# A retention and mixer kernel: batch 0 in the layout of the other batches, k turned back on TensorE, w2 cast by its DMA

## The chip, the core and the metric

The kernel runs on one core of a Trainium2 chip. A core has five engines with queues of their own: TensorE (PE; its weight loads are shown as PEld), VectorE (DVE), ScalarE (ACT), GpSimd (POOL) and SyncE (SP, which here only starts loads). Data lie in SBUF; matmuls write to PSUM, which has eight banks of 2 KB for each of 128 partitions. The metric is the device time of one execution in microseconds (us), as the median of several runs. The profile shows one execution of its own; times inside it count from the start of its span.

## What is computed

Four batches of 768 tokens with eight heads of width 64. A retention layer, written as a recurrence over the tokens, gives y; it is laid out as x with 512 columns. Then a low-rank mixing over the tokens is added, and a two-layer MLP with 2048 hidden columns:

```python
for t in range(S):
    state = gamma * state + k[:, :, t] (outer) v[:, :, t]
    y[:, :, t] = scale * q[:, :, t] @ state          # scale = 1/sqrt(64)
x = y.transpose(0, 2, 1, 3).reshape(B, S, H * D)
h = x.transpose(0, 2, 1) @ U @ V                     # rank 32
u = x + h.transpose(0, 2, 1)
out = u + relu(u @ w_ch1) @ w_ch2
```

Inputs and output are float32; the kernel multiplies in bf16 and accumulates in float32.

## The kernel before

**Retention by chunks.** A batch is cut into six chunks of 128 tokens. The decay is folded into q and into k or v as powers of gamma, so a chunk needs three products: scores of k against q within the chunk (masked to the causal part by DVE), the running state of k against v (kept in a PSUM bank "st" and copied to bf16 for the next chunk), and mix, which adds q times the state to the masked scores times v. Its result, x, is evacuated by ACT.

**Two layouts.** Batch 0 takes the first one: `prep_chunk` (L231) casts a chunk of q, k and v on POOL, `turn` (L266) transposes q and k on TensorE into a bank of PSUM, ACT copies them out as qkT, `score` (L293) and `mix` (L306) follow. Batches 1 to 3 take the head-pair layout: q and k are loaded with 32 partitions for each pair of heads and eight adjacent tokens in a partition (`feed_one`, L121, four DMAs of 128 KB for a tile of 256 tokens), cast by POOL (L211 and L215), and transposed in blocks of 32 by DVE (`turn_block`, L327). `score4` (L337) and `mix4` (L372) then work with a contraction over 32 partitions, four of them side by side. These batches also load k in its natural layout (L103), because the state needs tokens on the partitions.

**PSUM.** R (L63) is one tile of four banks, used by the retention and by the low-rank step; three banks "mlp" take turns in the MLP; one bank holds the state.

**Order.** The order of all instructions is written out by hand. SP starts the loads in the order of the list `feed` (L137 to L151); `take` and `feed_one` start the next load as one is used, with 19 tiles in flight at first. For batch 0 the loop at L519 runs turn of chunk ci, the casts of the next chunk, mix of chunk ci - 1 and score of chunk ci. Next come the casts of w1, the transposes of x for the first 512 tokens, the low-rank step (`lr_proj`, its copy pc on DVE, a product with V at L540, four evacuations to uT), and then the MLP of batch 0, whose first instruction is a matmul of L451. POOL meanwhile casts the first block of batch 1 and all of w2.

The MLP of a batch is a list of pieces: 16 up pieces of 512 tokens, 16 of 256 tokens (L451, with relu on ACT or DVE), and 24 down pieces of four matmuls each (L474). Every fourth down piece ends with an addition on DVE (L479) and a store, which POOL issues (L440). `weave` (L488) strews the next batch's retention and low-rank step between these pieces, at the shares of the total that stand in `AT` and `LR` (L551 to L557): for each block of 256 tokens the transposes, scores, mix, scores, mix; then projection (L403), sum (`lr_expand`, L412 and L419), and two turns of u into uT (`lr_turn`, L428, evacuated by ACT). All four read and write R.

Of the kernel before, what the change touches and what calls it, by code (L numbers as in the profile page):

```python
# [9 lines left out]
fp32 = mybir.dt.float32  # L10
# [3 lines left out]
ENG = mybir.EngineType  # L14
# [3 lines left out]
def kernel(  # L18
# [11 lines left out]
    nc = tc.nc  # L30
# [9 lines left out]
    RING = 19  # L40
    NBK = S // 256
    NST = 4
# [21 lines left out]
    Rb = R.bitcast(bf16)  # L64
# [28 lines left out]
    def feed_chunk(b, ci):  # L93
        for nm, src in (("q", q), ("k", k), ("v", v)):
            feed.append(((nm, b, ci),
                         src[b, :, ts(ci, P), :].rearrange("h p d -> p h d")))

    def feed_block(b, bk):
        for nm, src in (("qT", q), ("kT", k)):
            feed.append(((nm, b, bk), src[b, :, ts(bk, 256), :]))  # L100
        for ci in (2 * bk, 2 * bk + 1):
            for nm, src in (("k", k), ("v", v)):
                feed.append(((nm, b, ci),  # L103
                             src[b, :, ts(ci, P), :].rearrange("h p d -> p h d")))
# [32 lines left out]
    for ci in range(NCK):  # L137
        feed_chunk(0, ci)
# [4 lines left out]
    feed_block(1, 0)  # L143
    for m in range(NM):
        feed.append((("w2", m), moe_w_ch2[ts(m, P)]))
    for b in range(1, B):
        for bk in range(NBK):
            if (b, bk) != (1, 0):
                feed_block(b, bk)
    for _ in range(RING):  # L150
        feed_one()  # L151


    lg = consts.tile([P, NCK, H], fp32)
# [9 lines left out]
    for h in range(H):  # L164
        nc.vector.memset(lg[:, :, h], math.log(gammas[h]))
    nc.vector.tensor_tensor(pos, pos, lg, op=ALU.mult)
    gq = consts.tile([P, NCK, H], fp32)
    gk = consts.tile([P, NCK, H], fp32)
    nc.scalar.activation(gq, pos, AF.Exp)
    nc.scalar.activation(gk, pos, AF.Exp, scale=-1.0)  # L170
    nc.vector.tensor_scalar(gq, gq, 1.0 / math.sqrt(D), None, op0=ALU.mult)
# [4 lines left out]
    states = []  # L176
    for i in range(NST):
        t = consts.tile([P, 4, P], bf16, name=f"state{i}")
        nc.vector.memset(t, 0.0)
        states.append(t)  # L180

    def causal(t):
        return t[:, None, :].to_broadcast([P, 4, P])


    gqT = consts.tile([P, NBK, 8, 2], fp32)

    def make_gqT():
        lgT = consts.tile([P, NBK, 2, 8], fp32)
        posT = consts.tile([P, NBK, 2, 8], fp32)  # L190
        for hp in range(4):
            r = ds(32 * hp, 32)
            nc.gpsimd.iota(posT[r], pattern=[[256, NBK], [0, 2], [1, 8]], base=0,
                           channel_multiplier=8,
                           allow_small_or_imprecise_dtypes=True)
            for i in range(2):
                nc.gpsimd.memset(lgT[r, :, i], math.log(gammas[2 * hp + i]))
        nc.vector.tensor_tensor(posT, posT, lgT, op=ALU.mult)
        g = gqT.rearrange("p b a j -> p (b a j)")
        nc.scalar.activation(g, posT.rearrange("p b h j -> p (b h j)"), AF.Exp)  # L200
        nc.vector.tensor_scalar(g, g, 1.0 / math.sqrt(D), None, op0=ALU.mult)

    pre = {}

    def prep_block(b, bk):
        for nm in ("qT", "kT"):
            src = take(nm, b, bk).rearrange("p (a j d) -> p a j d", a=8, j=2)
            t = rblk.tile([P, 8, D, 2], bf16, tag=nm + "i", name=f"{nm}i_{b}_{bk}")
            dst = t.rearrange("p a d j -> p a j d")
            if nm == "qT":  # L210
                nc.gpsimd.tensor_tensor(  # L211
                    dst, src, gqT[:, bk, :, :, None].to_broadcast([P, 8, 2, D]),
                    op=ALU.mult)
            else:
                nc.gpsimd.tensor_copy(out=dst, in_=src)  # L215
            pre[nm, b, bk] = t
            feed_one()
        for ci in (2 * bk, 2 * bk + 1):
            t = rpre.tile([P, H, D], bf16, tag="kd", name=f"kd_{b}_{ci}")
            nc.gpsimd.tensor_copy(  # L220
                out=t, in_=take("k", b, ci).rearrange("p (h d) -> p h d", h=H))
            pre["k", b, ci] = t
            feed_one()
            t = rpre.tile([P, H, D], bf16, tag="vd", name=f"vd_{b}_{ci}")
            nc.gpsimd.tensor_tensor(  # L225
                t, take("v", b, ci).rearrange("p (h d) -> p h d", h=H),
                gk[:, ci, :, None].to_broadcast([P, H, D]), op=ALU.mult)
            pre["v", b, ci] = t
            feed_one()

    def prep_chunk(b, ci):  # L231
        for nm, g in (("q", gq), ("k", gk), ("v", None)):
            t = rpre.tile([P, H, D], bf16, tag=nm + "d", name=f"{nm}d_{b}_{ci}")
            src = take(nm, b, ci).rearrange("p (h d) -> p h d", h=H)
            if g is None:
                nc.gpsimd.tensor_copy(out=t, in_=src)
            else:
                nc.gpsimd.tensor_tensor(  # L238
                    t, src, g[:, ci, :, None].to_broadcast([P, H, D]),
                    op=ALU.mult)  # L240
            pre[nm, b, ci] = t
            feed_one()

    def prep_uv():
        take("uv")
        nc.gpsimd.tensor_copy(out=Ub, in_=Uf)
        nc.gpsimd.tensor_copy(out=V4, in_=Vf)
        feed_one()

    def prep_w1(mb):  # L250
        for c in range(NCB):
            nc.gpsimd.tensor_copy(out=w1b[:, c, ts(mb, 512)],  # L252
                                  in_=take("w1", mb, c))
            feed_one()

    def prep_w2(j):
        for m in range(4 * j, 4 * j + 4):
            nc.gpsimd.tensor_copy(out=w2b[:, m], in_=take("w2", m))  # L258
            feed_one()

# [3 lines left out]
    n_state = [0]  # L264

    def turn(b, ci, eng="D"):  # L266
        qd, kd, vb = (pre.pop((nm, b, ci)) for nm in "qkv")
        tp = Rb[:, 0]
        qkT = rmid.tile([P, 8, P], bf16, tag="qkT", name=f"qkT_{b}_{ci}", bufs=2)
        for p in range(4):  # L270
            nc.tensor.transpose(tp[:, ts(p, P)], qd[:, ds(2 * p, 2)], ident)  # L271
        for p in range(4):
            nc.tensor.transpose(tp[:, ts(4 + p, P)], kd[:, ds(2 * p, 2)], ident)  # L273
        evac(eng, qkT, tp.rearrange("p (n m) -> p n m", n=8))
        before = live.get(("state", b))
        if ci < NCK - 1:
            if ci == 0:
                live["st_p", b] = bank("st")
            st_p = live["st_p", b]
            for p in range(4):  # L280
                nc.tensor.matmul(st_p[:, ts(p, P)], kd[:, ds(2 * p, 2)],
                                 vb[:, ds(2 * p, 2)],
                                 start=(ci == 0 and p == 0), stop=True,
                                 skip_group_check=True)
# [329 lines left out]
```

## Time and profile before

| | before |
|---|---|
| median of 7 runs | 255.19 us (254.41 to 256.63) |
| the profiled execution | 256.33 us, its span 254.6 us |
| granted TensorE clock, mean | 0.984 |
| busy: PE, PEld | 219.8 us (86%), 122.9 us |
| busy: DVE, ACT, POOL | 105.9, 84.5, 109.5 us |
| loaded by SP's queue | 32.48 MB |
| first L451 matmul (MLP of batch 0) | 44.01 us |
| first L451 matmul of batch 1's MLP | 102.57 us |

The page gives shares of the whole span and cuts it into 40 equal slices, one digit for each, in tenths. The timeline lists an engine's instructions in order of time: start, duration, line, operation, tiles, and in brackets how long the engine had been idle and what released it. The chain of waits goes back from the last instruction to whatever released each step. A table by stretches gives the busy time of each engine, the granted clock, the busy share of the DMA engines and GB/s.

The costliest groups are the two products of the MLP, L451 with 91.5 us and L474 with 85.4 us; of the other engines, no single group has more than L458's 42.8 us (relu on ACT).

### The profile page before, as it was taken

The numbers are of one execution on the slowest core, as the hardware profiler recorded it, in microseconds if no ns is written. First come the engines' busy times: TensorE is split into PE (matmuls) and PEld (weight loads), VectorE is DVE, ScalarE is ACT, GpSimd is POOL, SyncE is SP. The second block draws the span as 40 slices with busy tenths as digits, with TensorE's granted clock in tenths as the row PEclk, the third lists the DMA queues.
The fourth block names the chain that finished last, engine by engine and source line by source line (L and its number), as shares of the span: only waits on it lengthen the run. The fifth ranks groups of instructions, "written<-read, shape, count | busy, mean of one in ns | idle before, by whom it ended". The sixth has DMA issues, their size and how long they took to land.

```text
span 254.6 us, 5508 instructions
## 1 busy us (share of the span) xinstructions
PE 219.8 (86%) x2257; PEld 122.9 (48%) x2284; DVE 105.9 (42%) x188; ACT 84.5 (33%) x159; POOL 109.5 (43%) x149
## 2 busy tenths in 40 slices
PE   0555655999999995899999999999999999999991
PEld 0444543345754443344764445447644444584440
DVE  3232223357434744276464353764633533231221
ACT  2444322255612112356641013565410135550000
POOL 4797575787648967454720921530001010000110
PEclk9999999999999998699999999999999999999999
DMA  8999799999999999998999522000011120001211
GB/s 164 218 218 217 225 364 267 233 356 311 214 206 229 264 229 244 222 275 200 231 205 243 134 82 82 3 0 3 4 44 59 68 82 1 0 3 41 80 53 76
DMA packets 69450, 39.14 MB, mean 154 GB/s; under 512 B 59056, under 2 KB 59056, under 8 KB 69424
## 3 DMA queue, kind: packets, MB, share of 16 engines
q1 hardware_dynamic: 67504, 32.48, 57.7%
q0 software_dynamic: 1920, 6.29, 6.6%
q8 instruction: 18, 0.29, 0.5%
q14 instruction: 8, 0.07, 0.1%
HBM read 32.47 MB, written 6.29 MB: 152 GB/s over the span
## 4 chain that ended last, share of the span: by engine, by line
PE 48%; issue 31%; SPq 8%; DMA 5%; POOL 3%; DVE 2%; ACT 2%; POOLq 0%; ACTq 0%; DVEq 0%
PE mlp L451 22%; PE mlp L474 15%; SPq L130 8%; POOL out_dram L440 2%; DMA Uf<-in_moe_U_dram 2%; DMA in<-in_moe_w_ch_dram 2%; PE r L345 2%; PE r L388 2%; PE r L428 2%; PE st L363 1%; ACT uT L76 1%; PE r L382 1%; PE r L412 1%; PE r L403 1%; DVE a L303 1%
## 5 line engine op out<-in xcount | busy, mean ns | idle before, releaser
L451 PE MATMUL mlp<-uT,w1b 128*128 128x256 bf16 (+1 forms) x503 | 91.5, 333 | 3.1 <-ACT uT L76 1.8
L474 PE MATMUL mlp<-w2b,gT 128*128 128x512 bf16 x366 | 85.4, 379 | 2.0 <-issue 1.6
L451 PEld LDWEIGHTS <-w1b 128*128 128x128 bf16 x512 | 48.9, 99 | 35.6 <-issue 7.5
L458 ACT ACTIVATE gT<-mlp 128x512 bf16<-128x512 f32 (+1 forms) x88 | 42.8, 490 | 45.7 <-PE mlp L451 43.8
L474 PEld LDWEIGHTS <-gT 128*128 128x128 bf16 x384 | 35.5, 98 | 39.1
L440 POOL DMA_DIRECT2D out_dram<-o x24 | 13.3, 555 | 87.2 <-DVE o L479 87.2
L456 DVE TENSOR_SCALAR gT<-mlp 128x512 bf16<-128x512 f32 (+1 forms) x40 | 22.3, 557 | 33.4 <-PE mlp L451 33.3
L479 DVE TENSOR_TENSOR o<-mlp,u 128x512 f32<-128x512 f32 x24 | 16.5, 689 | 44.1 <-PE mlp L474 43.2
L350 DVE TENSOR_TENSOR a<-r,mask 128x512 bf16<-128x512 f32 x36 | 23.2, 685 | 14.9 <-PE r L345 14.1
L225 POOL TENSOR_TENSOR vd<-in,gk 128x512 bf16<-128x512 f32 x18 | 18.7, 1041 | 19.2 <-PE r L388 12.1
L76 ACT ACTIVATE x<-r 128x512 bf16<-128x512 f32 x24 | 14.3, 597 | 33.7 <-PE r L388 27.7
L211 POOL TENSOR_TENSOR qTi<-in,gqT 128x1024 bf16<-128x1024 f32 x9 | 17.1, 1905 | 11.7 <-DMA in<-in_q_dram 4.8
L419 DVE TENSOR_TENSOR u<-r,x 128x512 bf16<-128x512 f32 (+1 forms) x16 | 14.6, 952 | 15.9 <-PE r L412 15.9
L76 ACT ACTIVATE uT<-r 128x1024 bf16<-128x1024 bf16 x10 | 10.2, 1023 | 26.4 <-PE r L428 26.4
L303 DVE TENSOR_TENSOR a<-r,mask 128x512 bf16<-128x512 f32 x12 | 7.7, 686 | 26.3 <-ACT x L76 13.9
L220 POOL CAST kd<-in 128x512 bf16<-128x512 f32 x18 | 11.0, 612 | 6.5 <-issue 3.8
L271 PE MATMUL r<-ident,qd 128*128 128x128 bf16 x24 | 3.5, 301 | 10.6 <-POOL qd L238 5.2
L215 POOL CAST kTi<-in 128x1024 bf16<-128x1024 f32 x9 | 12.0, 1331 | 1.1 <-DMA in<-in_k_dram 1.0
L76 ACT ACTIVATE qkT<-r 128x1024 bf16<-128x1024 bf16 x6 | 6.1, 1024 | 17.3 <-PE r L273 17.3
L252 POOL CAST w1b<-in 128x512 bf16<-128x512 f32 x16 | 9.8, 613 | 3.7 <-DMA in<-in_moe_w_ch_dram 3.4
L76 ACT ACTIVATE ns<-st 128x256 bf16<-128x256 f32 x15 | 5.8, 384 | 16.4 <-PE st L363 16.3
L258 POOL CAST w2b<-in 128x512 bf16<-128x512 f32 x16 | 9.8, 613 | 2.9 <-DMA in<-in_moe_w_ch_dram 2.3
(64 smaller groups left out, 149.5 us busy)
## 6 DMA issues: line engine op xcount, KB each, us to landing
in<-in_moe_w_ch_dram SPq DMA_DIRECT2D x32, 256.0 KB, 5.5
in<-in_k_dram SPq DMA_DIRECT2D x24, 256.0 KB, 5.4
in<-in_v_dram SPq DMA_DIRECT2D x24, 256.0 KB, 5.3
out_dram<-o POOLq DMA_DIRECT2D x24, 256.0 KB, 2.3
in<-in_q_dram SPq DMA_DIRECT2D x36, 128.0 KB, 4.8
in<-in_k_dram SPq DMA_DIRECT2D x36, 128.0 KB, 4.7
in<-in_q_dram SPq DMA_DIRECT2D x6, 256.0 KB, 5.1
Vf<-in_moe_V_dram SPq DMA_DIRECT2D x4, 96.0 KB, 4.2
```

Source lines behind the costliest of these rows:

```text
L76: nc.scalar.activation(dst, src, AF.Copy)
L130: nc.sync.dma_start(out=t, in_=src)
L211: nc.gpsimd.tensor_tensor(dst, src, gqT[:, bk, :, :, None].to_broadcast([P, 8, 2, D]), op=ALU.mult)
L225: nc.gpsimd.tensor_tensor(t, take("v", b, ci).rearrange("p (h d) -> p h d", h=H), gk[:, ci, :, None].to_broadcast([P, H, D]), op=ALU.mult)
L350: nc.vector.tensor_tensor(a[:, ds(4 * g, 4)].rearrange("p (n i) m -> p n i m", n=2), R[:, ds(2 * g, 2), :256].rearrange("p n (i m) -> p n ...
L419: nc.vector.tensor_tensor(v4(us[b][:, ds(j0, nj), e]), R[:, ds(2 * g, 2), :nj * P].rearrange("p c (j e) -> p c j e", j=nj), v4(xs[b][:, ds ...
L440: nc.gpsimd.dma_start(out=dst, in_=src)
L451: nc.tensor.matmul(g_p[:, :sz], w1b[:, c, ts(m, P)], uTs[b][:, c, ds(lo, sz)], start=(c == 0), stop=(c == NCB - 1))
L456: nc.vector.tensor_relu(gT[:, m, ds(lo, sz)], g_p[:, :sz])
L458: nc.scalar.activation(gT[:, m, ds(lo, sz)], g_p[:, :sz], AF.Relu)
L474: nc.tensor.matmul(ch, gT[:, m, ts(j, P)], w2b[:, m], start=(m == 0), stop=(m == NM - 1))
L479: nc.vector.tensor_tensor(o_sb, ch, us[b][:, j], op=ALU.add)
```

## The change

Batch 0 now takes the head-pair layout too. Its q and k are loaded in the turned form only; ACT casts its three k tiles, POOL its q tiles and all v but the last, which DVE casts. Where the state needs k in its natural layout, batches 0 and 1 get it from TensorE: `natural_k` multiplies the turned k with the identity into a bank "mlp", and ACT copies it out as kn. Batches 2 and 3 still load it. The factor 1/sqrt(64) goes into the exponent of the decay of q, the decay of k is folded into v everywhere.

`mix2` is a mix in two halves of two banks each, with an evacuation behind each half. The scores of batch 0's last chunk are computed beside chunk 4, three groups of them in "mlp" banks. The transposes of x and the first five sixths of the projection come before the last mix; the projection of batch 0 has the state's bank.

w2 is loaded by four DMAs from POOL's queue that cast to bf16 themselves. U, V and two tiles of w1 are cast by DVE instead of POOL. The order of loads and the shares for batch 1 are new; its state moves from `score4` to `mix4`. `lr_turn` uses plain matmuls into float32 banks.

```diff
+    HEAD = (("kT", 0), ("qT", 0), ("kT", 1), ("qT", 1), ("v", 0), ("v", 1),
+            ("kT", 2), ("qT", 2), ("v", 2), ("v", 3), ("v", 4), ("v", 5))
...
-    feed_block(1, 0)
-    for m in range(NM):
-        feed.append((("w2", m), moe_w_ch2[ts(m, P)]))
...
     for h in range(H):
-        nc.vector.memset(lg[:, :, h], math.log(gammas[h]))
...
+        r, lgh = ds(32 * (h // 2), 32), math.log(gammas[h])
+        nc.vector.tensor_scalar(
+            posT[r, :, h % 2], posT[r, :, h % 2],
+            -0.5 * math.log(D) / lgh - 256.0 * (h // 2), lgh,
+            op0=ALU.add, op1=ALU.mult)
...
+    for h in range(H):
+        nc.vector.tensor_scalar(pos[:, :, h], pos[:, :, h], math.log(gammas[h]),
+                                None, op0=ALU.mult)
...
-        nc.vector.memset(t, 0.0)
...
+    def prep_turned(nm, b, bk, eng="P"):
+        src = take(nm, b, bk).rearrange("p (a j d) -> p a j d", a=8, j=2)
+        t = rblk.tile([P, 8, D, 2], bf16, tag=nm + "i", name=f"{nm}i_{b}_{bk}")
...
+        cast(eng, t.rearrange("p a d j -> p a j d"), src, scale)
+        pre[nm, b, bk] = t
+        feed_one()
...
         for ci in (2 * bk, 2 * bk + 1):
+            if b > 1:
+                prep_natural("k", b, ci)
+            prep_natural("v", b, ci)
...
+    def load_w2(j):
+        nc.gpsimd.dma_start(
+            out=w2b[:, ds(4 * j, 4)],
+            in_=moe_w_ch2[ds(512 * j, 512)].rearrange("(m p) n -> p m n", p=P))
...
+    def scores(b, ci, groups, homes=None):
         qT, kT = bts["qT", b, ci // 2], bts["kT", b, ci // 2]
         tok = ts(ci % 2, P)
+        for hps in groups:
+            for i in range(2):
+                for c in range(2):
+                    for hp in hps:
+                        r = ds(32 * hp, 32)
+                        at = homes[hp] if homes else R[:, hp]
+                        nc.tensor.matmul(at[:, ts(i, P)], kT[r, i, c, tok],
+                                         qT[r, i, c, tok], start=(c == 0),
+                                         stop=(c == 1))
...
+    def natural_k(b, ci):
+        if ci == NCK - 1:
+            return
+        kT = bts["kT", b, ci // 2]
+        kp = bank("mlp")
         for i in range(2):
             for c in range(2):
...
+                nc.tensor.matmul(kp[:, ts(2 * i + c, P)],
+                                 kT[:, i, c, ts(ci % 2, P)], ident, start=True,
+                                 stop=True)
+        kn = rmid.tile([P, 4, 4, 32], bf16, tag="kn", name=f"kn_{b}_{ci}", bufs=2)
+        evac("A", kn.rearrange("p a n w -> p (a n w)"), kp)
+        live["kn", b, ci] = kn
...
+    def score4(b, ci):
+        if b == 1:
+            natural_k(b, ci)
+        scores(b, ci, (range(4),))
+        if b > 1:
+            state(b, ci)
...
     def mix4(b, ci):
...
+        if b == 1:
+            state(b, ci)
+        pre.pop(("v", b, ci))
         evac("A", four(xs[b][:, ci]), R[:, :, :P])
...
+    def mix2(b, ci, engines="AA"):
...
+        for g in range(2):
+            hps = (2 * g, 2 * g + 1)
...
+            evac(engines[g], four(xs[b][:, ci])[:, ds(2 * g, 2)],
+                 R[:, ds(2 * g, 2), :P])
...
     def lr_turn(b, j0, eng="A"):
-        tp = Rb[:, j0 // 2]
...
+        g = ds(j0 % 4, 2)
+        for c in range(NCB):
+            for jj in range(2):
+                nc.tensor.matmul(R[:, j0 % 4 + c // 2, ds(256 * (c % 2) + P * jj, P)],
+                                 us[b][:, j0 + jj, ts(c, P)], ident, start=True,
+                                 stop=True)
...
+    prep_turned("kT", 0, 0, "A")
+    prep_turned("qT", 0, 0)
+    for _ in range(13):
+        feed_one()
+    prep_turned("kT", 0, 1, "A")
+    turn_block(0, 0)
+    prep_turned("qT", 0, 1)
+    prep_natural("v", 0, 0)
+    prep_natural("v", 0, 1)
+    prep_turned("kT", 0, 2, "A")
+    prep_turned("qT", 0, 2)
+    for ci in range(LAST):
+        if ci < NCK - 2:
+            prep_natural("v", 0, ci + 2, "D" if ci == NCK - 3 else "P")
+        scores(0, ci, GR)
+        natural_k(0, ci)
+        if ci < 2:
+            turn_block(0, ci + 1)
+        if ci == LAST - 1:
             prep_uv()
...
+            homes = [bank("mlp") for _ in range(3)] + [R[:, 3]]
+            scores(0, LAST, ((0, 1), (2,)), homes)
+        state(0, ci)
+        mix2(0, ci)
+    scores(0, LAST, ((3,),), homes)
+    prep_w1(0, "PPDD")
+    x_turn(range(3))
+    p_p = bank("st")
+    proj(p_p, 0, range(LAST))
+    mix2(0, LAST, "AD")
+    x_turn((3,))
     lr_open(0)
-    lr_proj(0)
+    lr_proj(0, p_p, (LAST,))
...
+    for mb in range(1, 4):
+        prep_w1(mb)
+    load_w2(0)
+    load_w2(1)
     prep_block(1, 0)
-    for j in range(4):
-        prep_w2(j)
-
+    load_w2(2)
+    load_w2(3)
     prep_block(1, 1)
 
-    AT = {1: ((0.27, 0.32, 0.38, 0.42, 0.48), (0.56, 0.62, 0.67, 0.71, 0.76),
-              (0.74, 0.80, 0.84, 0.87, 0.91)),
+    AT = {1: ((0.36, 0.40, 0.45, 0.49, 0.53), (0.56, 0.60, 0.65, 0.69, 0.73),
+              (0.76, 0.79, 0.83, 0.86, 0.895)),
...
-    LR = {1: (0.94, 0.96, 0.98, 0.99), 2: (0.76, 0.80, 0.88, 0.92)}
+    LR = {1: (0.915, 0.935, 0.955, 0.975), 2: (0.76, 0.80, 0.88, 0.92)}
```

## The prediction

> **What bounds the kernel now.** I read the page first: busy shares, slices, shared chain.
>
> ```profile
> PE   0555655999999995899999999999999999999991
> ...
> PEclk9999999999999998699999999999999999999999
> DMA  8999799999999999998999522000011120001211
> ```
>
> TensorE is full from slice 8 on, except at slice 16. So there are two holes: the head (batch 0's retention, to 44.0 us, where the first L451 matmul starts) and a notch near 100 us. The DMA engines are busy to slice 23 (about 143 us), so whatever starts earlier must also have its data earlier.
>
> The timeline of TensorE in the head, one chunk:
>
> ```profile
> 27.46 0.58 PE L271 MATMUL r<-ident,qd 128*128 128x128 bf16 x4 [1.00 <-DVE a L303]
> ...
> 29.64 0.59 PE L313 MATMUL r<-state,qkT 128*128 128x128 bf16 x4 [0.73 <-ACT qkT L76]
> ...
> 31.33 0.61 PE L298 MATMUL r<-qkT 64*128 64x128 bf16 x8 [0.69 <-ACT x L76]
> ...
> 33.38 0.58 PE L271 MATMUL r<-ident,qd 128*128 128x128 bf16 x4 [1.00 <-POOL w1b L252]
> ```
>
> A chunk lasts 33.38 - 27.46 = 5.92 us. The matmuls wait for evacuations of banks that they don't touch: L313 writes bank 3 and starts as the evacuation of bank 0 (qkT) ends; L298 writes banks 1 and 2 and starts as the one of bank 3 (x) ends. R is followed as one tile, so a chunk is a serial chain. The last batch-0 loads are cast by 25.3 us; the chain, not DMA, ends the head.
>
> The chain of waits at the notch:
>
> ```profile
> 94.51 0.45 PE r L403 x24
> ...
> 97.46 1.23 DVE u L419
> ...
> 98.73 0.62 PE r L428 x8
> ...
> 100.45 1.03 PE r L428 x8
> ...
> 102.57 1.87 PE mlp L451 x4
> ```
>
> Batch 1's low-rank step (projection, sum u, two groups of transposes, two evacuations of 1.03 between them) has only two pieces of the down product beside it; then TensorE waits.
>
> **The change, part by part.** Times are from the span's start, from the rows of before.
>
> *Constants.* The state memsets (1.09 us on DVE, to 3.98) go; 16 small DVE operations come (the like, L201 and L166, took 0.2 to 0.6 us; beside each other less). They finish near 4.5 us, before the first q tile can be there. Cost 0.
>
> *Loads of the head.* Natural loads move 217 to 218 GB/s, 1.2 us each. A turned tile (512 KB) took 45.64 - 43.28 = 2.36 us between the landings of batch 1's q and k; single microseconds with such loads reach 296 GB/s (133 to 134 us), which is 1.8 us. I take 2.05. From natural landings (the second at 5.2 us = 2.8 + 2 x 1.2), the third k tile lands at 2.8 + 5 x 2.05 + 2 x 1.2 = 15.4 us (ends 14.2 and 17.0). On SP the third k tile waits for the cast of the first (near 6) and the third q tile, with v, U, V and w1 behind it, for POOL's cast of the first q (near 9.5): both are over before the queue of about 1 MB ahead has drained. Cost 0; with no backlog there, a landing of about 4.8 us.
>
> *The first chunk.* ACT's order puts the casts of all three k tiles ahead of the first natural-k evacuation, so that stands behind the DMA of the third k tile; TensorE's state matmuls wait for it, and mix stands behind them. 15.4 + cast 1.02 (as qkT, same size) + kn 0.60 + state 0.5 + two halves of mix and x, 2 x (0.40 + 0.43) = 19.2 us for the scores of chunk 1. POOL's v is ready earlier: q1 near 11.3, then 1.9 and 1.04.
>
> *A chunk.* Scores, two masks (1.29), half mix, x evacuation (0.384, the ns row), half mix, x evacuation, one after the other, because R is still one tile. With TensorE at full clock: 0.53 (L345 to L350) + 1.34 + 0.33 + 0.43 + 0.33 + 0.43 = 3.4. In the head of before L403 took 0.83 for what took 0.52 later, so its matmuls ran slower there although the clock column reads 1.00; with such: 0.71 + 1.34 + 0.62 + 0.43 + 0.62 + 0.43 = 4.15. I take 3.8. Natural k, kn and state lie beside the masks. On DVE the transposes of block 2 stand ahead of the mask of chunk 2 and end near 23.7, when it is due; the cast of the last v (landed at 22.3) stands ahead of that of chunk 3: 0. So the scores of chunk 4 start at 19.2 + 3 x 3.8 = 30.6, and its x is out 4.2 later (it carries most of chunk 5's scores), 34.8.
>
> *The tail.* Last score group and mask 0.9; transposes and projection beyond that 1.2; mix in two halves 1.8; last projection 0.6; from pc to the first L451 1.64, as before. Together 6.1: the MLP starts at 40.9 instead of 44.0: **-3.1** (ends -7 and +1). The casts of U, V and two of w1 on DVE (about 0.6 each, as L78) lie beside TensorE's transposes; uncovered, they'd cost 2.
>
> *w2 by its DMA.* 16 casts (9.8 us of POOL) and 16 issues of SP go. POOL's queue: w1 casts to about 37 us, two w2 loads, block 0 of batch 1, two more, block 1. The row: 16 loads of w2 took 9.91 us to issue, 2.5 us per MB. Block 0's loads take 6.5. The Trainium skill ("DMA: Bandwidth & Descriptors", the part on one DMA of the GpSimd path) says about 2.0 us plus bytes at 436 GB/s, 4.4 us per MB, and (on issuing engines) that all queues share the same 16 engines: no bandwidth is won, and batch 1's loads are slowed by w2's. By the row the first pair and block 0 are in at 48, POOL is through at 50, the second pair and block 1 are in at 62; by the page 52, 54 and 69. The down product starts at 40.9 + 28 = 69 (26.8 us after the MLP's start before, plus what this part adds) and reaches the second pair's rows at 70.6. Either way 0. No trace row shows a casting load, so its rate is a rival below.
>
> *k of batch 1.* Six loads (1.57 MB, 7.2 us of DMA) and six casts go; hidden work, 0. In place come five times four matmuls (L428's eight add 0.45, so 0.23) on the full TensorE: **+1.2**. The kn evacuations (0.6) have room in ACT, which is at 33%.
>
> *Later marks of batch 1.* A down piece lasts 0.86. Transposes of a block keep DVE 2.07 us (58.58 to 60.65). Before, three pieces lie between them and the scores. Now one does in block 2 (stall 1.25), two in block 1 (0.4), four small ones in block 0 (0.7). Mix of chunk 5 comes one piece after its scores: the mask is out 1.9 after they start, cover 1.2, stall 0.7. Behind each stalled matmul stands the MLP itself. **+3.0** (ends 1 and 4.5).
>
> *The notch.* The projection now has four pieces behind it. From its start: sum 4 done at 0.85, pc 1.15, expand 1.3, both u sums out at 4.15, while TensorE's work ends at 2.5: idle 1.7. First transposes, evacuation, second transposes (waiting for it, R again): idle 0.4. First L451 at 7.6, idle 0.4. Sum 2.5. Before: 8.06 from projection to L451, of which 3.4 was work: 4.65 idle or slow. And then the slow clock:
>
> ```profile
> 100.00:102.00 2.00, 1.01 (x8) 0.85 (x8) 0.00 (x0) 0.90 (x2) 1.39 (x2) 0.50 1.38 220
> 102.00:104.00 2.00, 1.43 (x4) 0.41 (x3) 0.00 (x0) 0.52 (x1) 0.94 (x3) 0.50 1.13 231
> 104.00:106.00 2.00, 1.67 (x13) 0.61 (x13) 1.11 (x2) 0.60 (x1) 1.83 (x3) 0.50 1.09 236
> 106.00:108.00 2.00, 2.00 (x15) 1.10 (x14) 0.56 (x2) 0.60 (x1) 0.00 (x0) 0.82 1.19 199
> ```
>
> These are the stretches behind the notch; the third figure from the end is the granted clock. The eleven L451 matmuls from 102.57 on took 4.34 instead of 2.4: 2.3 with what follows. The skill ("TensorE: Matmul & The Clock Gate", Part 1) halves the clock after one idle window of about 3.4 us. By the rule gaps of 1.7, 0.4 and 0.4 keep it full: saving 2.15 + 2.3 = 4.4. The trace lost it to three gaps of 1.5, 1.1 and 1.1; by that, the new gaps might do it too: saving 2.1, and the time would be 254.2. From 98 to 102 TensorE was 40% busy, in the new notch 51%; I side with the rule: **-4.4** (ends -6 and -2).
>
> *The rest.* Plain matmuls for the transposes of L428 have the same columns and evacuation size: 0. Batches 2 and 3 keep their marks: 0.
>
> **Sum:** -3.1 + 1.2 + 3.0 - 4.4 = -3.3. Against the profiled execution (256.33, span 254.6): 253.0, span 251.3. The median of the runs is 1.1 below that execution; 255.19 - 3.3 = **251.9 us**.
>
> **Rivals.** *Short head:* full clock (3.4 per chunk) and k tiles at 1.8 us start the MLP near 37.5, and DVE is free at the marks: 251.9 - 3.4 - 1.5 = 247. For: bursts of 296 GB/s. Against: L403's 0.83 in the head.
>
> *No difference:* chunks at 4.15 and late k (MLP at 43.5) with a slow clock after the notch: 251.9 + 2.6 + 2.2 = 256.7 at worst, 255 with one and a half of these. For: the single-tile R. Against: both must hold.
>
> *Slower, by w2:* the second pair of w2 loads stands in POOL's queue behind block 0's casts, which wait for loads that share the engines with the first pair. A pair (2.1 MB) at 215 GB/s takes 9.8 us and is just in time; below that rate the down product of batch 0 waits, microsecond for microsecond, twice per pair. At 150 GB/s (14 us a pair) it is in at 79 for pieces due at 70.6: 251.9 + 8.4 = 260. For: a casting load is new here. Against: plain w2 loads ran at 356 GB/s.
>
> **Chances.** A measurement tells 0.5% (1.3 us) from no change. Forecast (249.5 to 253.9) 0.47, short head 0.23, no difference 0.14, w2 late 0.16. Faster 0.70, same 0.14, slower 0.16. The range 246 to 256.5 leaves out the w2 case and little below.
>
> **What would show it.** First L451 near 41; kTi of the third tile as the last thing ahead of the first kn on ACT; chunks of 3.4 to 4.15 us, L379's second half waiting for x; TensorE gaps before the scores of batch 1's chunks 0, 2, 4; clock 1.00 after the next notch, which falls near 99. Wrong: an L474 that waits for w2's DMA, or a head that ends on loads.

## The result, and the profile after

The changed kernel takes **258.83 us** (median of 12 runs, 257.96 to 259.17); the kernel before, run beside it on the same chip, takes 255.19 us (31 runs). The ratio is 1.0128, 95% interval 1.0105 to 1.0151: slower, by 3.6 us, where 3.3 us less had been forecast. (A ratio leaves out runs more than 1.5% above the fastest of the same kernel; that matters for two experiments below, whose own times spread that far.) The profiled execution of the changed kernel took 258.56 us, its span 256.8 us, at a mean granted clock of 0.998.

The three rows of the page, in 40 slices of 6.42 us:

```profile
PE   0205677799999997899999999999999999999991
...
PEclk9999999999999999999999999999999999999999
...
DMA  7999999999999999949693112000011220001211
```

Both holes are still there, and they changed in opposite ways. The head (slices 0 to 7, counted from 0) has become longer: TensorE is nearly idle in slice 2 and at 0.5 to 0.7 after it. The notch (slices 15 and 16, before 5 and 8, now 7 and 8) has become shallower, and the clock row, which had a dip behind the notch before, stays at 9.

Three marks split the span: the first matmul of batch 0's MLP (L455 now), the first of batch 1's MLP, the end.

| stretch, us | before | forecast | after |
|---|---|---|---|
| start to the MLP of batch 0 | 44.01 | 40.9 | 47.65 |
| MLP of batch 0, with the notch | 58.56 | 60.6 | 58.89 |
| from the MLP of batch 1 to the end | 152.0 | 149.7 | 150.2 |
| span | 254.6 | 251.3 | 256.8 |

(60.6 is 58.56 + 1.2 + 3.0 - 2.15; 149.7 is 152.0 - 2.3.) The head alone is 6.75 us over its forecast, the rest 1.2 us under it. The medians lie further apart than the spans (3.6 against 2.2) because the profiled execution of before was 1.1 us above its median, that of after 0.3 below.

Line numbers differ from kernel to kernel. In the changed kernel L270 is the scores, L286 their mask on DVE, L298 natural k, L324 the state, L379 and L385 the two products of `mix2`, L353 and L359 those of `mix4`, L73 an evacuation by ACT, L401 the projection, L422 the sum u, L431 the turn of u, L455 and L478 the two products of the MLP.

**The first chunk.** The timeline of ACT after, then TensorE's natural k and the matmuls that wait for its copy:

```profile
9.78 1.35 ACT L192 ACTIVATE kTi<-in 128x1024 bf16<-128x1024 f32 x1 [3.38 <-DMA in<-in_k_dram]
16.97 1.33 ACT L192 ACTIVATE kTi<-in 128x1024 bf16<-128x1024 f32 x1 [5.85 <-DMA in<-in_k_dram]
18.18 0.57 ACT L73 ACTIVATE kn<-mlp 128x512 bf16<-128x512 f32 x1
```

```profile
12.11 0.61 PE L298 MATMUL mlp<-ident,kT 128*128 128x128 bf16 x4
18.80 0.40 PE L324 MATMUL st<-vd,kn 128*32 128x64 bf16 x16 [6.08 <-ACT kn L73]
```

Natural k of chunk 0 was complete in its bank at 12.7 us. Its copy kn stands on ACT behind the cast of the third k tile, and that cast waits for its load until 16.97. ACT does nothing for 5.85 us, and TensorE, which needs kn for the state, does nothing for 6.08.

**A chunk in the middle.** The timeline of all engines after, in order of time (start, duration, engine, line; in brackets how long the engine had been idle and until what):

```profile
30.29 0.64 PE L270 MATMUL r<-qT,kT 32*128 32x128 bf16 x16 [0.47 <-ACT x L73]
...
30.86 0.61 PE L298 MATMUL mlp<-ident,kT 128*128 128x128 bf16 x4
...
31.57 0.60 ACT L73 ACTIVATE kn<-mlp 128x512 bf16<-128x512 f32 x1 [1.32 <-PE mlp L298]
...
32.55 0.40 PE L379 MATMUL r<-ns,qT 32*128 32x64 bf16 x8
...
33.31 0.38 ACT L73 ACTIVATE x<-r 128x256 bf16<-128x256 f32 x1 [0.26 <-PE r L385]
33.75 0.40 PE L379 MATMUL r<-ns,qT 32*128 32x64 bf16 x8 [0.47 <-ACT x L73]
...
34.51 0.38 ACT L73 ACTIVATE x<-r 128x256 bf16<-128x256 f32 x1 [0.81 <-PE r L385]
34.94 0.64 PE L270 MATMUL r<-qT,kT 32*128 32x128 bf16 x16 [0.47 <-ACT x L73]
```

From scores to scores 34.94 - 30.29 = 4.65 us, of which 32.55 - 30.29 = 2.26 us lie ahead of the mix. The second half of the mix (33.75) writes two banks that the first half doesn't use, and waits 0.47 us for the first half's evacuation all the same; then the next scores wait for the second. Each half costs 1.2 us (1.20 and 1.19), one after the other.

**The notch.** The chain of waits after:

```profile
98.89 0.45 PE r L401 x24
...
101.84 1.22 DVE u L422
...
103.11 0.62 PE r L431 x8
...
104.82 0.62 PE r L431 x8
...
106.54 1.02 PE mlp L455 x4
```

From projection to MLP 7.65 us, with pieces of the down product beside both evacuations. Four matmuls of L455 take 1.02 us here; before, the first four took 1.87. The table by stretches (PE, PEld, DVE, ACT, POOL busy; clock, DMA share, GB/s) shows the granted clock at 1.00, where before it was 0.50:

```profile
102.00:104.00 2.00, 0.90 (x11) 0.73 (x12) 1.05 (x1) 0.25 (x1) 0.00 (x0) 1.00 1.02 302
104.00:106.00 2.00, 1.75 (x15) 1.00 (x14) 0.00 (x0) 1.30 (x2) 0.00 (x0) 1.00 1.10 228
```

### The profile page after: what moved, and what is told of

Read it like the earlier page. It is cut to its first block, busy times and chain, and to the rows that moved or that the text cites. A ratio compares the mean times of both kernels' runs of the same rounds, so it can differ in the third digit from the quotient of the medians.

```text
span 256.8 us, 5778 instructions
## 1 busy us (share of the span) xinstructions
PE 218.9 (85%) x2416; PEld 121.2 (47%) x2444; DVE 113.5 (44%) x208; ACT 86.5 (34%) x165; POOL 90.7 (35%) x106
## 4 chain that ended last, share of the span: by engine, by line
PE 59%; issue 20%; DMA 7%; SPq 4%; DVE 3%; ACT 3%; POOL 2%; POOLq 0%; DVEq 0%; ACTq 0%
PE mlp L455 25%; PE mlp L478 20%; DMA in<-in_k_dram 3%; PE r L270 3%; PE r L359 2%; SPq L122 2%; SPq L131 2%; DMA Uf<-in_moe_U_dram 2%; DMA in<-in_moe_w_ch_dram 2%; PE st L324 2%; POOL out_dram L444 2%; PE r L353 1%; PE r L431 1%; ACT uT L73 1%; DVE u L422 1%
## 5 line engine op out<-in xcount | busy, mean ns | idle before, releaser
L455 PE MATMUL mlp<-uT,w1b 128*128 128x256 bf16 (+1 forms) x503 | 89.2, 328 | 1.9 <-ACT uT L73 0.9
L478 PE MATMUL mlp<-w2b,gT 128*128 128x512 bf16 x365 | 86.1, 379 | 2.0 <-issue 1.4
L455 PEld LDWEIGHTS <-w1b 128*128 128x128 bf16 x512 | 48.6, 98 | 33.7 <-issue 3.5
L478 PEld LDWEIGHTS <-gT 128*128 128x128 bf16 x384 | 35.3, 98 | 38.8
L286 DVE TENSOR_TENSOR a<-r,mask 128x512 bf16<-128x512 f32 x46 | 29.6, 685 | 28.1 <-PE r L270 22.1
L198 POOL TENSOR_TENSOR vd<-in,gk 128x512 bf16<-128x512 f32 x23 | 23.8, 1040 | 27.3 <-PE r L359 10.5
L198 POOL TENSOR_TENSOR qTi<-in,gqT 128x1024 bf16<-128x1024 f32 x12 | 22.9, 1909 | 20.7 <-DMA in<-in_q_dram 12.9
L73 ACT ACTIVATE x<-r 128x512 bf16<-128x512 f32 (+1 forms) x29 | 14.9, 515 | 29.2 <-PE r L359 20.9
L270 PE MATMUL r<-qT,kT 32*128 32x128 bf16 x372 | 11.4, 235 | 13.5 <-DVE kT L255 11.1
L422 DVE TENSOR_TENSOR u<-r,x 128x512 bf16<-128x512 f32 (+1 forms) x16 | 14.6, 953 | 10.9 <-PE r L415 10.9
L73 ACT ACTIVATE uT<-r 128x1024 bf16<-128x1024 f32 x10 | 10.2, 1023 | 25.0 <-PE r L431 25.0
L255 DVE STREAM_TRANSPOSE qT<-qTi 128x256 f32<-128x256 f32 x24 | 13.2, 624 | 8.8 <-POOL qTi L198 6.9
L270 PEld LDWEIGHTS <-kT 32*128 32x128 bf16 x384 | 7.6, 100 | 20.0 <-DVE kT L255 11.4
L73 ACT ACTIVATE ns<-st 128x256 bf16<-128x256 f32 x20 | 7.7, 384 | 20.6 <-PE st L324 20.4
L255 DVE STREAM_TRANSPOSE kT<-kTi 128x256 f32<-128x256 f32 x24 | 12.9, 615 | 0.0
L324 PE MATMUL st<-vd,kn 128*32 128x64 bf16 x160 | 3.5, 218 | 8.3 <-ACT kn L73 7.5
## 6 DMA issues: line engine op xcount, KB each, us to landing
w2b<-in_moe_w_ch_dram POOLq DMA_DIRECT2D x4, 512.0 KB, 11.1
```

Of the source, the lines that this page charges most:

```text
L73: nc.scalar.activation(dst, src, AF.Copy)
L198: e.tensor_tensor(dst, src, scale, op=ALU.mult)
L255: nc.vector.transpose(out=dst[:, i], in_=src[:, i])
L270: nc.tensor.matmul(at[:, ts(i, P)], kT[r, i, c, tok], qT[r, i, c, tok], start=(c == 0), stop=(c == 1))
L286: nc.vector.tensor_tensor(pair_view(a[:, ds(4 * g, 4)], 2), R[:, ds(2 * g, 2), :256].rearrange("p n (i m) -> p n i m", i=2), mask[:, None, ...
L422: nc.vector.tensor_tensor(v4(us[b][:, ds(j0, nj), e]), R[:, ds(2 * g, 2), :nj * P].rearrange("p c (j e) -> p c j e", j=nj), v4(xs[b][:, ds ...
```

## The experiments

Two theories stood at the start. The first: the head is long for two reasons of order, the k cast in front of kn on ACT, and the mix in halves on a tile that is followed as one. The second: the head ends on something that no order mends (the loads of the turned tiles, or natural k), or the loss is further back (marks, w2's DMA, natural k on a full TensorE). All kernels start from the changed one unless it is said otherwise. A ratio is to the kernel before, run beside each experiment; its median there lay between 255.2 and 255.9 us. A difference from the changed kernel is one of medians, and so is good to about 0.7 us.

### The k cast behind the first mix

```diff
-    prep_turned("kT", 0, 2, "A")
-    prep_turned("qT", 0, 2)
...
-        if ci < NCK - 2:
+        if 0 < ci < NCK - 2:
             prep_natural("v", 0, ci + 2)
...
+        if ci == 0:
+            prep_turned("kT", 0, 2, "A")
+            prep_turned("qT", 0, 2)
+            prep_natural("v", 0, 2)
```

> The changed kernel with one move: ACT's cast of the third k tile, with the q tile and v that follow it, stands behind the mix of chunk 0 instead of ahead of the first kn. Theory 1 (the head is late because the first kn stands behind the third k tile's DMA): kn of chunk 0 runs near 12.8 us instead of 18.2, mix of chunk 0 near 15.2 instead of 19.1, and the mask of chunk 2, now held by the transposes of block 2, at 23.5 instead of 26.6; the first L455 matmul near 44.6 instead of 47.7, about 3 us less in all, near 255.7. Rival (the chunk chain alone sets the head; the first chunk's wait is taken back by the wait for block 2's transposes): less than 1 us.

Measured: 255.74 us, 1.0003 of before (0.9982 to 1.0024), so 3.1 us less than the changed kernel. TensorE's timeline:

```profile
15.10 0.40 PE L324 MATMUL st<-vd,kn 128*32 128x64 bf16 x16 [2.54 <-POOL vd L198]
...
17.15 0.64 PE L270 MATMUL r<-qT,kT 32*128 32x128 bf16 x16 [0.47 <-ACT x L73]
...
24.66 0.40 PE L379 MATMUL r<-ns,qT 32*128 32x64 bf16 x8 [0.60 <-DVE a L286]
```

The state starts at 15.10 instead of 18.80, now released by POOL's v. The scores of chunk 1 come 3.7 us earlier, the MLP 2.8 (44.81). About half of what is lost on the way goes in chunk 2 (0.46 us), whose mask now waits on DVE behind transposes of a block whose q POOL casts later; the rest goes in the tail, where the last transposes of x wait 0.99 us for DVE instead of 0.58. The edit moves a q tile and a v on POOL too, but the wait that went is ACT's: the place of the k cast in its queue cost 3 us by itself.

### The mix in one piece

```diff
-        for g in range(2):
-            hps = (2 * g, 2 * g + 1)
+        for g in range(1):
+            hps = (0, 1, 2, 3)
...
-            evac(engines[g], four(xs[b][:, ci])[:, ds(2 * g, 2)],
-                 R[:, ds(2 * g, 2), :P])
+            evac(engines[g], four(xs[b][:, ci]), R[:, :, :P])
```

> The changed kernel with batch 0's mix in one group of all four head pairs and one evacuation by ACT, instead of two halves. Theory 1 (R is followed as one tile, so the halves only line up: two times 0.76 for the matmuls and 0.43 for the evacuation): one group takes about 1.05 + 0.65, so a chunk falls from 4.7 to about 4.0 us and the first L455 comes near 43.5 instead of 47.7; about 4 us less, near 255. Rival (the halves do overlap with something, mask or scores): a chunk of 4.7 or more, no gain.

Measured: 253.75 us, 0.9924 (0.9901 to 0.9947), 5.1 us less than the changed kernel. One chunk on TensorE:

```profile
27.99 0.64 PE L270 MATMUL r<-qT,kT 32*128 32x128 bf16 x16 [0.69 <-ACT x L73]
...
30.25 0.40 PE L379 MATMUL r<-ns,qT 32*128 32x64 bf16 x16
...
30.59 0.61 PE L385 MATMUL r<-vd,a 128*128 128x64 bf16 x8
31.88 0.64 PE L270 MATMUL r<-qT,kT 32*128 32x128 bf16 x16 [0.68 <-ACT x L73]
```

Sixteen L379 matmuls over all four groups of partitions take no longer (0.40) than eight over two did, and the pair of evacuations (0.38 each) is one of 0.60. The period falls from 4.65 to 3.89, and the tail, with two such mixes, from 12.7 to 11.1 (31.88 to 42.95). So cutting the mix in halves made it longer: nothing of one half could lie beside the other.

### R as two tiles

R becomes two tiles of two banks, so that the halves can really overlap. Of the other steps only the evacuation of `mix4` spanned all four banks; it is cut in two to fit.

```diff
-    R = psum.tile([P, 4, 512], fp32, tag="r", name="r")
+    RR = [psum.tile([P, 2, 512], fp32, tag=f"r{g}", name=f"r{g}") for g in range(2)]
...
-        evac("A", four(xs[b][:, ci]), R[:, :, :P])
+        for g in range(2):
+            evac("A", four(xs[b][:, ci])[:, ds(2 * g, 2)], RR[g][:, :, :P])
```

> The changed kernel with R as two tiles of two banks; mix of batches 1 to 3 gets two evacuations in place of one, all else is the same. Theory 1 (a wait on the whole of R makes the halves serial): the second half of mix doesn't wait for the first x evacuation, a chunk takes about 3.6 us instead of 4.7, the first L455 comes near 42.5, and in the notch before batch 1's MLP the second group of transposes doesn't wait for the first evacuation (0.9 us less): 5 to 6.5 us less, near 253. Rival (the halves are ordered by the engines' queues, kn and state ahead of mix): less than 2 us.

Measured: 254.36 us, 0.9951 (0.9934 to 0.9969), 4.5 us less than the changed kernel. TensorE:

```profile
22.80 0.39 PE L383 MATMUL r<-ns,qT 32*128 32x64 bf16 x8
23.12 0.39 PE L389 MATMUL r<-vd,a 128*128 128x64 bf16 x4
23.45 0.40 PE L383 MATMUL r<-ns,qT 32*128 32x64 bf16 x8
```

The second half follows without a wait: the wait was the one tile. The gain is not above that of the whole mix: the scores, 0.64 before, now take 1.15 us (the second evacuation ends 0.5 us after they start, and their second half writes the banks that it reads), so natural k, its copy and the state start later, and the period is 4.08. The MLP starts at 44.31, with the whole mix at 42.95. In the notch, where the first turn of u now waits for one of the two sums only, gaps of 0.35 and 0.74 us stand in place of 1.49. All in all the halves gain nothing over the simpler form.

### Old marks for batch 1

```diff
-    AT = {1: ((0.36, 0.40, 0.45, 0.49, 0.53), (0.56, 0.60, 0.65, 0.69, 0.73),
-              (0.76, 0.79, 0.83, 0.86, 0.895)),
+    AT = {1: ((0.27, 0.32, 0.38, 0.42, 0.48), (0.56, 0.62, 0.67, 0.71, 0.76),
+              (0.74, 0.80, 0.84, 0.87, 0.91)),
...
-    LR = {1: (0.915, 0.935, 0.955, 0.975), 2: (0.76, 0.80, 0.88, 0.92)}
+    LR = {1: (0.94, 0.96, 0.98, 0.99), 2: (0.76, 0.80, 0.88, 0.92)}
```

> The changed kernel with the shares of before for batch 1's steps. Theory of the prediction: the stalls before batch 1's scores go (3 us less), but the notch before batch 1's MLP grows by 2.2 us and the clock halves there again (2.3 us): 1.5 us slower, near 260. Rival (the later marks only shift work): the same within 0.5 us. A second rival: the shares of before come too early for the loads of batch 1, which now share the engines with w2, and DVE waits in its transposes: 3 us slower or more.

Measured: 261.68 us, 1.0248 (1.0199 to 1.0297), 2.9 us more than the changed kernel. The notch on TensorE, and the stretches of two microseconds there:

```profile
103.68 0.61 PE L431 MATMUL r<-ident,u 128*128 128x128 bf16 x8 [1.49 <-DVE u L422]
105.40 0.62 PE L431 MATMUL r<-ident,u 128*128 128x128 bf16 x8 [1.11 <-ACT uT L73]
107.13 1.87 PE L455 MATMUL mlp<-uT,w1b 128*128 128x512 bf16 x4 [1.11 <-ACT uT L73]
```

```profile
102.00:104.00 2.00, 0.51 (x7) 0.41 (x7) 2.00 (x3) 0.00 (x0) 0.74 (x2) 1.00 1.15 228
104.00:106.00 2.00, 0.89 (x14) 0.65 (x11) 0.22 (x1) 1.02 (x1) 0.54 (x1) 0.96 1.04 271
106.00:108.00 2.00, 0.89 (x4) 0.32 (x3) 0.00 (x0) 1.02 (x1) 0.00 (x0) 0.50 1.06 302
```

The first gap is the same 1.49 us in both kernels. What the new marks shorten are the two of 1.11 behind it, to 0.25 each, and the slow clock goes with them. The time is that of the second rival, but its cause is excluded: with the old marks the timeline lists no wait of TensorE between 48 and 102 us. The loss is above 1.5 us because the stalls that the old marks save were about 1.0 us (0.54 and 0.49, below) and not 3.0.

### New marks on the kernel before

The same exchange the other way round, in the kernel before and in nothing else of it.

> The kernel before with only the new shares for batch 1's steps. Theory of the prediction: stalls before batch 1's scores cost 3.0 us, the notch before batch 1's MLP shrinks by 2.2 and the clock stays full behind it, which saves 2.3 more: 1.4 us faster, near 253.8, with a granted clock of 1.00 throughout. Rival (the marks bring only the stalls): 2 to 3 us slower. Rival (neither): the same.

Measured: 252.80 us, 0.9873 (0.9831 to 0.9915). The kernel before, beside it, had 255.93, so these shares alone take 3.1 us off, about as much as they are worth in the changed kernel (2.9). The stalls that I had charged to them came to 0.66 us (0.50 before the mix of the last chunk, 0.16 before one group of scores).

### w2 loaded by SP and cast by POOL

```diff
-    load_w2(0)
-    load_w2(1)
...
-    load_w2(2)
-    load_w2(3)
+    for j in range(4):
+        prep_w2(j)
```

> The changed kernel with w2 as before: 16 loads on SP's queue behind block 0 of batch 1, 16 casts on POOL. Theory of the prediction (w2 by its DMA is hidden either way): the same time within 1 us, and the down product of batch 0 waits for nothing in either. Rival (w2's DMA, in flight beside batch 1's loads, delays these and so DVE's transposes): 1.5 to 4 us faster.

Measured: 258.65 us, 1.0100 (1.0064 to 1.0135), the time of the changed kernel within the noise (0.2 us less by the medians, 0.7 by the ratios): how w2 is loaded makes no difference that these runs show, and the rival that made its rate the cause falls.

### k of batch 1 loaded again

```diff
-            if b > 1:
+            if b > 0:
                 prep_natural("k", b, ci)
...
-        if b == 1:
-            natural_k(b, ci)
```

> The changed kernel with batch 1's k loaded in natural layout and cast by POOL, its state in the scores step, as before; batch 0 keeps natural k from TensorE. Theory of the prediction (natural k costs TensorE 0.23 us a chunk on the full engine): 1.2 us faster. Rival (the loads of 1.57 MB come back just where batch 1's transposes wait for q and k): no gain, or 1 to 3 us slower.

Measured: 256.97 us, 1.0042 (1.0025 to 1.0059), 1.9 us less than the changed kernel. From natural k to the scores behind it TensorE needs 0.31 to 0.48 us a chunk after the change, 1.75 us for the five of batch 1, where 1.2 had been forecast; and a stall of 0.54 us at L298 goes with it.

### Both mends of the head, and DVE's transposes

The late cast and the whole mix together; then, in a second kernel, the transposes of block 2 moved behind the mask that they had held up.

```diff
-        if ci < 2:
-            turn_block(0, ci + 1)
+        if ci in (0, 2):
+            turn_block(0, ci // 2 + 1)
```

> The changed kernel with both edits of the head: the third k tile's cast behind chunk 0, and batch 0's mix in one group with one evacuation. If the two add up: 3.1 + 5.1 us less, near 250.6. Theory (they overlap, since the mask of chunk 2 then stands on DVE behind the transposes of block 2, which wait for the third q tile, landed at 19.5 us, and POOL's 1.9): mask of chunk 2 at 23.5, the first L455 near 41.3, about 1.7 us better than with the one group alone, near 252.

> As the run before, and the transposes of block 2 (for chunks 4 and 5) come on DVE behind the mask of chunk 2 instead of chunk 1. Theory: chunk 2 no longer waits for them, chunks of 3.9 us from the first mix on, the first L455 near 39.3: another 2 us, near 250. Rival (block 2's transposes then come too late for the scores of chunk 4, or chunk 2 never waited): no gain.

Measured: 252.13 us, 0.9838 (0.9792 to 0.9885), and 251.53 us, 0.9813 (0.9764 to 0.9863). The two mends overlap: 3.1 and 5.1 us alone, 6.7 together, because chunk 2, starting earlier, meets DVE's transposes, which still wait for q (1.56 us of waiting before its mix). Moving these brought 0.6 us, not the 2 that I expected, and four runs of each kernel hardly tell that from nothing; the start of the MLP moved by as much (41.29 and 40.70). The next wait, 0.91, is for chunk 3's mask, which stands on DVE behind the cast of the last v, and that behind its load.

### With k of batch 1 loaded, and the notch earlier

On top of the last kernel, batch 1's k is loaded again (worth 1.9 us above); then the last marks move forward as well.

```diff
-              (0.76, 0.79, 0.83, 0.86, 0.895)),
+              (0.74, 0.78, 0.82, 0.85, 0.875)),
...
-    LR = {1: (0.915, 0.935, 0.955, 0.975), 2: (0.76, 0.80, 0.88, 0.92)}
+    LR = {1: (0.895, 0.915, 0.955, 0.975), 2: (0.76, 0.80, 0.88, 0.92)}
```

> As the run before, and batch 1's k loaded in natural layout (the edit that took 1.8 us off the changed kernel). If TensorE's time is what it saved: another 1.2 to 1.8 us, near 248.5. Rival (the MLP now starts 8 us earlier, so the extra 1.57 MB make batch 1's q and k late): no gain or slower, with TensorE waiting for DVE's transposes of batch 1.

> As the run before, with block 2 of batch 1 and its low-rank step one piece earlier, so that two pieces stand between the sum u and the first transposes: the idle 1.5 us before these in the notch falls to about 0.6, about 1 us less, near 247.5. Rival (block 2's data or masks come too late for the earlier marks): no gain.

Measured: 255.5 us (20 runs, 252.7 to 258.3) and 255.66 us (20 runs, 251.1 to 257.8), ratios 0.9947 (0.9916 to 0.9978) and 0.9901 (0.9863 to 0.9939). Both are a miss: an edit that had won 1.9 us now lost 4.0 by the medians and 3.4 by the ratios, and the runs no longer agree. The earlier notch brought nothing that can be told from noise. The chain of waits of the first of the two, in an execution that took 257.44 us, 1.9 above its median:

```profile
77.69 7.22 DMA in<-in_v_dram
...
85.07 0.98 POOL vd L198
86.06 5.83 DMA out_dram<-o
...
91.97 0.06 DVE o L478
...
93.18 0.69 DVE a L286
...
93.91 0.40 PE r L351 x13
```

A load of v takes 7.22 us to land. POOL waits for it in order to cast it, and behind that cast in POOL's queue stand stores of finished rows. The store goes out at 86.06 and takes 5.83 us; DVE needs its tile for the next sum and has only three of them; behind that sum stands a mask; and behind the mask TensorE, which waits 3.87 us. (The rival had TensorE wait for transposes of q and k; that wait is 0.16 us.) In the profiled execution of the second kernel DVE waits 6.55 us for a store, and TensorE 4.24. In the gap the clock halves as well:

```profile
92.00:94.00 2.00, 0.09 (x9) 0.09 (x12) 1.86 (x3) 0.00 (x0) 1.07 (x2) 0.50 0.70 167
94.00:96.00 2.00, 2.00 (x28) 1.01 (x27) 0.00 (x0) 0.60 (x1) 0.59 (x1) 0.50 0.94 250
96.00:98.00 2.00, 2.00 (x28) 0.84 (x27) 0.98 (x2) 0.00 (x0) 1.56 (x2) 0.50 0.73 173
```

### Six output tiles

This chain is read from a trace, so it was tested by changing one number in the first of these two kernels.

```diff
-    outp = ctx.enter_context(tc.tile_pool(name="outp", bufs=3))
+    outp = ctx.enter_context(tc.tile_pool(name="outp", bufs=6))
```

> The kernel with the late k cast, the whole mix and k of batch 1 loaded, with one number changed: six output tiles o instead of three. In its profile with three, TensorE stood 3.87 us at 90 us for a mask of DVE; DVE stood 6.2 us in front of the fourth sum o, whose tile was still waiting for its store; and the store stood in POOL's queue behind casts of v that waited for their loads. Theory (a chain through POOL's queue and the output tiles): with six tiles DVE doesn't wait for a store in batch 0's MLP, the 3.87 us go, the wait of the down product for w2 (1.7 us) stays. Span about 251.5, time 253 us, and the runs lie closer together than 252.7 to 258.3. Rival (the loads of batch 1 are simply late, so the scores or the mix wait for data whatever the output tiles are): the gap of 3 to 4 us stays in front of another instruction and the median stays near 255.5.

Measured: **251.11 us** (six runs, 249.9 to 255.3), 0.9837 (0.9791 to 0.9882). The profiled execution has a span of 247.9 us, 3.6 below what I expected, and the gap is gone:

```profile
88.48 0.30 PE L351 MATMUL r<-ns,qT 32*128 32x64 bf16 x16 [0.50 <-DVE a L286]
```

The median is 4.4 us lower than with three tiles (by the ratios 2.8), so the chain through the output tiles was what the two kernels above had lost by: the loads of v in this stretch took as long as with three (median 6.8 us to landing, 6.7 there), and the stores went out at 84.78, 1.3 us earlier, but no sum waited for them. The one other wait that a short head brings, of the down product for w2's DMA, is 0.59 us here (1.71 with three tiles). One of the six runs still took 255.3; what delayed it isn't known. Against the kernel without the loaded k (251.53) the median is no gain that can be told from noise, so the 1.9 us of that edit were not seen again; that kernel with six tiles was not run.

## Why the prediction was wrong

**The step that failed is the head, -3.1 forecast and +3.64 measured.** All three of its terms were too small:

- *The first chunk:* scores of chunk 1 at 20.84 instead of 19.2. The mechanism was right and written down: kn behind the cast, the cast behind its load. Its size was at my late end: the third k tile came near 16.9 instead of 15.4 (ends 14.2 and 17.0), since a turned tile took 2.2 to 2.5 us where I took 2.05 (between the row of 2.36 and a burst; the row was right). The cast took 1.33 instead of 1.02. And I treated this wait as a fact of the load. The late cast shows it was one of order, worth 3.7 us at that point.
- *The period:* 4.59, 4.86 and 4.65 instead of 3.8, above my upper end of 4.15. I had priced each half of the mix at full or half clock plus an evacuation (0.76 to 1.05) and got 1.19: eight L379 and four L385 matmuls take 0.76 us from start to evacuation, against 0.33 to 0.62 in the sum. And I let natural k, kn and state "lie beside the masks"; from scores to mix they need 2.26 us (30.29 to 32.55), where I had 2.05 for scores and masks. The whole mix has a period of 3.89: what I forecast is what the head does without the cut.
- *The tail:* 12.7 us from the scores of chunk 4 instead of 10.3. Chunk 4 took 5.1 instead of 4.2; the last scores, the transposes and the projection 2.6 instead of 2.1; the last mix 2.4 instead of 1.8; the last projection 0.9 instead of 0.6; from there to the MLP 1.64 as forecast. Two of these hold a mix in halves; with whole ones the tail is 11.1. For the other 0.8 us there is no experiment.

1.64 + 2.70 + 2.41 make up the 6.75 us. I had seen that R is one tile and that the halves would run one after the other, and still counted the cut as a part of a shorter chunk, instead of asking what the same mix uncut would take. That the change's shares for batch 1 were worth 2.9 us, more than the 1.4 they had in the sum, hid a part of the head's loss.

**Right or nearly so.** The notch: 7.65 us against 7.6, its first gap shorter (1.49 against 1.7). The clock behind it: the rule of the Trainium skill ("TensorE: Matmul & The Clock Gate", Part 1), by which I chose, forecast 1.00 for the change, and the trace has 1.00; but other runs contradict the rule (last section), so the choice was in part luck. From the MLP of batch 1 to the end it took 1.8 us less, where 2.3 were forecast. w2's DMAs were hidden, though not at the estimated rate: each reads 1 MB and took 8.4 to 14.0 us from issue to landing, beside loads of SP's queue. The row of before had given 2.5 us for each MB, the figure of the Trainium skill ("DMA: Bandwidth & Descriptors", on one DMA of the GpSimd path) 4.4, an estimate for one that is alone; no run shows that.

**Wrong in two smaller terms.** Natural k of batch 1 was priced at 1.2 us, by half of what eight L428 matmuls add (0.45), and took 1.75, the four L298 matmuls of a chunk 0.31 to 0.48. The stalls of the later marks, 3.0 us forecast, were 0.54 and 0.49:

```profile
68.08 0.38 PE L298 MATMUL mlp<-ident,kT 128*128 128x128 bf16 x4 [0.54 <-DVE gT L460]
...
97.39 0.30 PE L353 MATMUL r<-ns,qT 32*128 32x64 bf16 x16 [0.49 <-DVE a L286]
```

The first is a wait of natural k for a bank "mlp": it is not there with the old marks, nor where batch 1's k is loaded. I let DVE's transposes start at their mark in TensorE's list. Its timeline after shows that for block 2 they start as the sum o before them is done, so nearly all of their 2 us were over when natural k (90.24) and the scores (90.72) came:

```profile
87.81 0.69 DVE L483 TENSOR_TENSOR o<-mlp,u 128x512 f32<-128x512 f32 x1 [0.46 <-PE mlp L478]
88.41 1.11 DVE L255 STREAM_TRANSPOSE qT<-qTi 128x256 f32<-128x256 f32 x2
89.36 1.09 DVE L255 STREAM_TRANSPOSE kT<-kTi 128x256 f32<-128x256 f32 x2
```

**The rivals.** "No difference" had the right mechanism, slow chunks and late k, but put the worst at 256.7 because it took both at their ends (4.15 and 17.0) and let neither go beyond. "Slower, by w2" would have given the right sign for a reason that the kernel with SP's loads excludes. No rival put the period above 4.15 us or the tail above 10.3.

## What to carry to other kernels

Cutting a step in two helps only if the halves can overlap: find out by what unit the waits are made, and price the uncut form beside the cut one. In a queue that runs in order, a job that waits for a load holds up every job behind it, so an early cast is free only if nothing that is due sooner stands behind it; what such a delay costs is found by following each queue to the next, here from a load over a cast, a store, an output tile and a mask to TensorE. When a stage becomes shorter, the next limits (loads, buffers of the outputs) come due earlier by the same time, so an edit that won alone can lose in its company.

## What the runs showed of the hardware

TensorE ran at about half speed in the head while the granted clock reads 1.00 there. Two pairs of rows from one execution (the kernel before with the new marks), the head first:

```profile
41.37 0.83 PE L403 MATMUL r<-x,Ub 128*32 128x128 bf16 x24 [0.69 <-ACT x L76]
...
43.95 3.39 PE L451 MATMUL mlp<-uT,w1b 128*128 128x512 bf16 x8 [0.68 <-ACT uT L76]
...
93.12 0.52 PE L403 MATMUL r<-x,Ub 128*32 128x128 bf16 x24
...
102.02 1.90 PE L451 MATMUL mlp<-uT,w1b 128*128 128x512 bf16 x8
```

With k of batch 1 loaded, the same projection fell into a stretch with a granted clock of 0.50 (96 to 98, shown above), and took what it takes in the head:

```profile
96.49 0.83 PE L396 MATMUL r<-x,Ub 128*32 128x128 bf16 x24
```

The changed kernel shows the same (four L298 matmuls: 0.61 us at 30.86, 0.39 at 73.45). A chunk in the head is to be priced by rows of the head.

The slow clock doesn't need one long gap. With the old marks in the changed kernel, gaps of 1.49 and 1.11 us had brought it to 0.50 by 106, TensorE being busy for 1.40 of the 4 us before; the change's gaps of 1.49, 0.25 and 0.25, with 2.65 of 4 us busy, left it at 1.00. Nor does it wait for a gap to have a certain length: in the gap of 3.87 us, which begins at 90.05, the clock fell at about 91.8, after 1.8 us, and in the gap of 4.24 us of the kernel with the earlier notch after about 3.3. (Worked out from the granted clock by stretches: 1.00 up to 91.8 and 0.60 from there to 92.0; in the other kernel 1.00 up to 93.2 and 0.50 from there, TensorE idle since 89.87.) So the rule that I used, one idle window of about 3.4 us, is not the whole of it. These runs agree with a measure of how busy TensorE was over some microseconds, but don't fix how it is taken or where it turns.
